# One linear-attention and MLP kernel on one core: reciprocals by a head-major round trip through DRAM, five more tile transposes by DMA, one load for the keys' weight, and a new order of the work

## The chip, the core and the metric

The kernel runs on one core of one Trainium2 chip. The metric is device time in microseconds for one execution; the kernel before took 170.77 us, the median of 3 runs (170.71 to 170.78). The core has five engines with queues of their own: TensorE (PE in the profile, with its weight loads as PEld), VectorE (DVE), ScalarE (ACT), GpSimd (POOL) and SyncE (SP). An engine takes its instructions strictly in the order of the program and waits on semaphores; SP issues all DMAs of this kernel.

## The reference

A block of linear attention with 32 heads of width 16, and behind it a two-layer MLP, both with a layernorm in front and a residual. The sequence has 2048 rows of 512 columns, the MLP is 1792 wide, all data are bfloat16.

```python
def _A_ref(x, wqkv, wo):
    q, k, v = qkv[0], qkv[1], qkv[2]
    phi = lambda t: jnp.where(t > 0, t + 1, jnp.exp(t)) + 1e-6
    pq, pk = phi(q), phi(k)
    kv = jnp.einsum("bhsd,bhse->bhde", pk, v)
    z = jnp.einsum("bhsd->bhd", pk)
    num = jnp.einsum("bhqd,bhde->bhqe", pq, kv)
    den = jnp.einsum("bhqd,bhd->bhq", pq, z)[..., None] + 1e-6
    o = num / den
    return o.transpose(...).reshape(B, S, D) @ wo
...
h = x + _A_ref(_layernorm(x, axis=-1), A_wqkv, A_wo)
h2 = h + _B_ref(_layernorm(h, axis=-1), B_w1, B_w2)    # _B_ref: relu(x @ w1) @ w2
```

## The kernel before

The rows are cut into 16 tiles of 128 (`t`) and 4 blocks of 512 (`c`, four tiles each). Nothing is scheduled by a planner while it builds: the string `ORDER` (lines 18 to 55) lists all steps, a loop at its end (L523) calls `op_<name>` with the numbers behind the name, and each engine runs its part in that order. So `K.4.0` is `op_K(4, 0)`: tile 4, PSUM bank 0. The eight PSUM banks are one tile, `bk`, and the last number of most PE steps names the bank.

The steps, in the order in which they mostly come:

- `lx` loads tiles of x, `lk`, `lq`, `lv`, `lo`, `l1`, `l2` load the weights (L212, L215). `lk.0.2` and `lk.2.2` are the two halves, 256 KB each, of the keys' weight. `warm` (L226) runs PE on zeros.
- Layernorm 1: `S`, `A` (statistics and mean, L229, L230), `R` (1/sqrt by Ln and Exp on ACT), `N` (L243, into `h_nat`).
- A tile must be transposed before it can be multiplied by a weight. It is done either by `T` on PE (four passes against the identity, L262) with a copy out of PSUM by `E` (ACT) or `V` (DVE), or by `X`, a transpose by DMA issued from SP (L283). Before, tiles 0 to 5 go over PE, tiles 6 to 15 by DMA, into `lnT`, one tensor for each block.
- `K` (L291): the keys of a tile, four passes of 512 columns. `F` (exp, L309), `U` (relu, L312), `M` (L316), `D` (L319) make phi of them. `G` (L343) gathers LN(x)^T times phi(k) in four banks over all 16 tiles.
- z, the sum of phi(k) over all rows: `za` (L351) adds tiles 2 to 13 two by two on DVE; `z` (L366) adds the rest on PE, six parts (two for the sum, tiles 0, 1, 14, 15) for each of four blocks of columns, so 24 passes of one column.
- `Q` (L299), `qF`, `qU`, `qM`, `qD`: phi(q), transposed. `kv`, `kx`, `m` make the product of the masked kv and `wo` (L388, L396, L400), so that attention's output is phi(q), scaled by the reciprocals, times `m_sb`.
- The reciprocals, by block: `d4` (L414) makes the denominators, four passes that share the array; row `32 j + h` holds head h (of 8) of column block j. `dl4`, `dx4` (L420, L425) take exp(-ln). Each must then stand on 16 rows, those of its head. For block 0 that is done on PE: `rp` (L430) multiplies by the matrix `erep`, one pass for each of four banks, and `rm` (L436) multiplies out of PSUM. For blocks 1 to 3 it goes through DRAM: `wb` (L442) writes 128 rows of 512 to `scr`, and eight loads `rb` (L445), one for each h, read 4 rows 16 times over into 16 rows of `rr`; then `dm` (L452) multiplies. `rr` exists once, so a block's loads wait until the block before has been multiplied.
- `h` (L461, four passes), `hD` (L467, the residual); layernorm 2 with `s`, `a`, `r`, and `n` (L250), which only subtracts the mean, since 1/sqrt is multiplied in at the end. The transposes of `hn` are again by PE (`t`, L262, with copies `v`) or by DMA (`x`, L284): before, tiles 1, 2, 3 by PE and the others by DMA.
- `p` (L476; `ph`, L485, is half a block) multiplies by w1, `pA` (ACT, L491) and `pD` (DVE, L496) apply relu, `f` (L505) multiplies by w2, `fo` (L513) adds the residual and `fd` (L520) stores.

A DMA waits on SP, so whatever stands behind it in `ORDER` and is issued by SP waits too. DMAs use eight semaphores in turn, and one also waits for that eight DMAs ahead.

Of the kernel before, what the change touches and what calls it, by code (L numbers as in the profile page):

```python
# [15 lines left out]


ORDER = """
table const masks warm.70.7.64 warm.3.7 lx.1.1 S.1 lx.0.1 S.0 lx.3.1 lx.2.1 lx.4.2 A.1 S.3 A.0 R.1.1 R.0.1 S.2
A.3 N.1 A.2 N.0.0.2 N.0.2.2 S.5 R.2.2 T.0.0.0.2 T.0.3.2.2 T.1.1 warm.1.7 E.0.2.2 E.0.0.2 lk.0.2 lk.2.2 N.3  # L20
T.3.3 A.5 S.4 N.2 A.4 lx.6.2 K.0.0 T.2.2 E.1 K.1.1 R.4.2 V.3 F.0.1 U.0.1 F.1.1 U.1.1 V.2 K.2.2 N.4 T.4.0 F.2.1
E.4 M.0.1 N.5 lx.8.4 D.0.1 S.6 S.7 M.1.1 A.6 A.7 D.1.1 S.8 R.6.2 G.0 T.5.1 K.3.3 K.4.0 E.5 G.1 K.5.1 U.2.1
F.3.1 U.3.1 N.7 S.9 A.8 N.6 M.2.1 A.9 M.3.1 D.2.1 R.8.2 lx.12.4 X.7 X.6 F.4.2 U.4.2 G.2 D.3.1 N.8 S.13 N.9
A.13 M.4.2 S.12 D.4.2 A.12 R.12.2 G.3 K.7.3 K.6.2 X.8 X.9 lq.0.2 F.6.2 U.6.2 G.4 K.8.0 S.11 S.10 A.10 N.13
A.11 M.6.2 N.12 K.9.1 R.10.2 U.8.2 F.8.2 D.6.2 X.13 X.12 S.15 N.10 A.15 S.14 A.14 N.11 M.8.2 D.8.2 R.14.2 N.15
N.14 za.4 X.10 X.11 lq.2.2 X.15 X.14 lv.0.2 l1.2.2 lv.2.2 l2.7.7 lo.0.2 lo.2.2 l1.0.2 G.5 G.6 G.7 K.13.1
K.12.0 G.8 K.10.2 K.11.3 F.12.2 U.12.2 F.10.2 U.10.2 Q.0.0.0 Q.0.1.1 G.9 qU.0.0.2 M.12.2 za.6 M.10.2 D.12.2
D.10.2 za.8 za.10 K.14.2 K.15.3 G.10 G.11 G.12 G.13 F.14.2 U.14.2 qF.0.0.2 Q.0.2.0 M.14.2 za.12 D.14.2 G.14 zf
G.15 zhi zlo qM.0.0.2 qD.0.0.2 z.2.2 z.0.2 z.1.2 Q.0.3.1 z.3.2 zc gA.0.2 Q.1.1.3 Q.1.0.2 gD.2.2 qF.0.2.2
qU.0.2.2 qF.1.0.2 qU.1.0.2 kv.2.4 kv.1.4 kv.3.4 kv.0.4 qM.0.2.2 zh qD.0.2.2 qM.1.0.2 kx qD.1.0.2 Q.1.3.1  # L30
Q.1.2.0 qF.1.2.2 m.2.6 m.3.7 d4.0.3 m.0.4 m.1.5 mD.2.2 mD.0.2 Q.2.0.2 dl4.0 dx4.0 qU.1.2.2 Q.2.1.3 rp.0.3.7
rp.0.0.4 rp.0.1.5 rp.0.2.6 Q.2.2.0 Q.2.3.1 qM.1.2.2 rm.0.0.2 rm.0.2.2 h.0.4 qD.1.2.2 hD.0 h.1.5 h.3.7 qU.2.0.2
qU.2.2.2 qF.2.0.2 qF.2.2.2 d4.1.4 h.2.6 dl4.1 dx4.1 Q.3.2.0 Q.3.3.1 s.0 hD.1 a.0 hD.3 s.1 n.0 a.1 hD.2 n.1 s.3
s.2 a.3 qU.3.2.2 qF.3.2.2 x.0 wb.1 rb.1.2 rb.1.4 rb.1.6 rb.1.0 rb.1.7 rb.1.5 rb.1.3 rb.1.1 l2.0.7 a.2 n.3
Q.3.1.3 t.1.5 Q.3.0.2 n.2 v.1 t.3.7 t.2.6 v.3 v.2 ph.0.3.1.0 ph.0.2.0.0 ph.0.3.1.1 ph.0.2.0.1 qF.3.0.2
qU.3.0.2 pA.0.2.2 ph.0.0.2.1 ph.0.0.2.0 ph.0.1.3.1 ph.0.1.3.0 p.0.6.0 p.0.7.1 pD.0.6.2 dm.1.0.2 dm.1.2.2
qM.2.2.2 qM.2.0.2 pA.0.0.2 p.0.5.3 p.0.4.2 p.0.11.1 p.0.10.0 h.6.6 qM.3.0.2 pA.0.4.2 hD.6 h.4.4 h.5.5 p.0.9.3
h.7.7 p.0.8.2 pA.0.8.2 f.2.6.0.7 qD.3.0.2 qD.2.2.2 hD.5 qM.3.2.2 hD.4 s.6 qD.2.0.2 qD.3.2.2 a.6 n.6 hD.7 s.5
s.4 a.4 s.7 a.5 n.4 a.7 p.0.13.3 p.0.12.2 r.0.4 pD.0.12.2 pA.0.10.2 d4.2.0.2 dl4.3 dx4.3 f.0.4.0.7 dl4.2 dx4.2
f.1.5.0.7 n.5 n.7 f.3.7.0.7 f.0.4.7.7 f.2.6.7.7 f.1.5.7.7 x.4 x.7 wb.2 x.5 x.6 p.1.1.1 p.1.0.0 rb.2.0 rb.2.4  # L40
rb.2.6 rb.2.1 wb.3 rb.2.5 fo.0 rb.2.7 rb.2.2 rb.2.3 p.1.2.2 p.1.3.3 pD.1.0.2 p.1.5.1 p.1.4.0 pA.1.4.2 r.4.4
pD.1.2.2 fo.2 dm.2.2.2 dm.2.0.2 f.3.7.7.7 p.1.8.0 p.1.6.2 h.10.6 hD.10 fo.1 fd.1 fo.3 rb.3.6 rb.3.2 rb.3.7
p.1.7.3 h.8.4 pA.1.6.2 p.1.9.1 h.11.7 hD.8 f.4.4.0.7 p.1.10.2 hD.11 s.10 s.11 a.11 n.11 pA.1.8.2 p.1.13.1
h.9.5 hD.9 s.9 a.9 f.7.7.0.7 p.1.11.3 a.10 s.8 rb.3.3 rb.3.0 rb.3.4 rb.3.1 rb.3.5 p.1.12.0 pA.1.10.2 pA.1.12.2
f.5.5.0.7 f.7.7.7.7 n.10 n.9 a.8 r.8.4 x.9 fd.2 dm.3.2.2 dm.3.0.2 n.8 fd.3 fd.0 fo.7 x.8 x.10 x.11 f.6.6.0.7
f.5.5.7.7 h.15.7 fo.5 f.6.6.7.7 p.2.0.0 h.13.5 p.2.1.1 f.4.4.7.7 p.2.2.2 fo.6 pA.2.0.2 p.2.4.0 h.14.6 p.2.3.3
pA.2.2.2 hD.15 hD.13 s.15 fo.4 p.2.5.1 h.12.4 p.2.7.3 pA.2.4.2 p.2.6.2 hD.14 s.13 p.2.8.0 p.2.9.1 hD.12 s.14
a.15 a.13 s.12 a.14 a.12 pD.2.6.2 r.12.4 n.15 pA.2.8.2 n.14 n.13 n.12 x.13 fd.7 fd.6 x.15 fd.5 x.14 x.12
f.11.7.0.7 f.10.6.0.7 f.9.5.0.7 p.2.12.0 p.2.11.3 p.2.10.2 p.2.13.1 pD.2.10.2 pA.2.12.2 f.8.4.0.7 f.9.5.7.7
p.3.0.0 p.3.1.1 f.10.6.7.7 pA.3.0.2 p.3.3.3 p.3.5.1 p.3.4.0 p.3.2.2 pA.3.4.2 f.8.4.7.7 p.3.9.1 pD.3.2.2  # L50
p.3.6.2 p.3.8.0 f.11.7.7.7 p.3.7.3 fo.11 pA.3.8.2 fo.9 fd.4 fo.10 fo.8 p.3.12.0 p.3.13.1 pD.3.12.2 fd.10 fd.9
pA.3.6.2 f.13.5.0.7 p.3.11.3 p.3.10.2 pD.3.10.2 f.12.4.0.7 f.15.7.0.14.0.2 f.12.4.7.7 fd.8 fd.11 f.14.6.0.7
f.13.5.7.7 fo.15.0.2 fo.12 fo.13 fd.12 fd.13 fd.15.0.2 f.14.6.7.7 fo.14 fd.14 f.15.5.0.14.3.1 fo.15.3.1
fd.15.3.1 f.15.4.0.14.2.1 fo.15.2.1 fd.15.2.1
"""


# [1 line left out]
def kernel(  # L59
# [10 lines left out]
    nc = tc.nc  # L70
# [55 lines left out]
    h_nat = big.tile([P, NT, D], BF16, name="h_nat")  # L126
# [16 lines left out]
    mv2 = big.tile([P, NT, nc.vector.BN_AGGR_DIM], F32, name="mv2")  # L143
    rstd2 = big.tile([P, NT], F32, name="rstd2")
    eb = big.tile([P, NE, 2, CW], BF16, name="eb")
    rb = big.tile([P, NE, 2, CW], BF16, name="rb")
    ld = big.tile([P, NCH, CW], F32, name="ld")
    rd = big.tile([P, NCH, CW], BF16, name="rd")
    rr = big.tile([P, KD, CW], BF16, name="rr")
    scr = [dram.tile([KD, Q4, 1, CW], BF16, name=f"scr{c}") for c in range(NCH)]  # L150
    pqs = big.tile([P, NQ, CW], BF16, name="pqs")
    hn = big.tile([P, NQ, D], BF16, name="hn")
    o_t = gT
# [87 lines left out]
    def op_N(t, k=0, n=KD):  # L241
# [106 lines left out]
    def op_za(t):  # L350
# [10 lines left out]

    def op_z(jb, b):
        at_bank["z"] = b
        parts = [zhl[:, i, :] for i in range(2)] + [pk(t)[:, 0, :] for t in range(NT) if not 2 <= t < ZT + 2]
        for i, part in enumerate(parts):
            nc.tensor.matmul(  # L366
                bk[:, b, jb : jb + 1], lhsT=part[:, jb * P : (jb + 1) * P], rhs=ones[:],
                start=(i == 0), stop=(i == len(parts) - 1),
            )
# [131 lines left out]
    def op_f(t, b, f0, n, k=0, w=KD):
# [54 lines left out]
```

## Time and profile before

| | us |
|---|---|
| time, median of 3 runs | 170.77 |
| span of the profiled execution | 169.2 |
| PE busy | 163.5 |
| DVE busy | 101.0 |
| ACT busy | 65.4 |
| load of `wk_sb`, second half, landed | 8.54 |
| first pass of `h.0` starts | 50.16 |
| last DMA landed | 168.40 |

The profile is of one execution; its span is 1.57 us shorter than the median time of the runs, which also holds what lies ahead of the first and behind the last instruction. A group of instructions is shown by line, engine and operation, with its busy time, its count, the mean time of one, and what it waited for. A chain of waits is followed back from the last instruction and then printed in order of time. All times inside the span count from its start.

### The profile page before, as it was taken

The page shows a single profiled execution, that of the slowest core. Times are in us where ns is not written, and L with a number is a line of the kernel's source. Part 1 is how long each engine was busy: PE and PEld are TensorE (multiplying, and loading weights), DVE is VectorE, ACT ScalarE, POOL GpSimd, SP SyncE. Part 2 cuts the span into 40 slices and gives each one's busy share as a digit, 9 for nine tenths or more (in the row PEclk, how much of TensorE's full clock was granted, in tenths as well). Part 3 has the DMA queues.
Part 4 walks back from the last instruction along what each step waited for, and adds up shares of the span by engine and source line. Part 5 has one row for each costly group of instructions (what it writes and reads, how often), then busy time and mean ns, then how long its engine had stood idle before and what let it go on. Part 6 is the DMA issues. An engine that isn't in the chain of part 4 may idle for free.

```text
span 169.2 us, 2376 instructions
## 1 busy us (share of the span) xinstructions
PE 163.5 (97%) x906; PEld 79.9 (47%) x922; DVE 101.0 (60%) x208; ACT 65.4 (39%) x96; POOL 4.7 (3%) x21
## 2 busy tenths in 40 slices
PE   7799999999999999999999999999999999999993
PEld 7454444445534674434444444444444444444643
DVE  3989997896899908895127567326481200255323
ACT  3689766656878672055003222302232112140000
POOL 7300000000000000000000000000000000000000
PEclk9999999999999999999999999999999999999999
DMA  5952656896000246002440031530005500004003
GB/s 135 279 210 50 111 119 153 281 364 259 1 2 4 62 133 208 0 4 59 104 147 2 18 94 48 155 62 0 0 0 97 124 31 0 0 0 127 1 31 93
DMA packets 23163, 15.10 MB, mean 89 GB/s; under 512 B 13808, under 2 KB 22128, under 8 KB 23152
## 3 DMA queue, kind: packets, MB, share of 16 engines
q1 hardware_dynamic: 23152, 14.95, 31.3%
q8 instruction: 7, 0.11, 0.3%
q14 instruction: 4, 0.03, 0.1%
HBM read 9.44 MB, written 2.49 MB: 70 GB/s over the span
## 4 chain that ended last, share of the span: by engine, by line
PE 91%; DMA 3%; SPq 1%; issue 1%; DVE 1%
PE bk L505 29%; PE bk L476 26%; PE bk L343 8%; PE bk L461 8%; PE bk L291 8%; PE bk L299 7%; DMA wk_sb<-in_A_wqkv_dram 3%; PE bk L485 2%; SPq L212 1%; PE bk L262 1%; DVE pqs L436 1%; PE bk L414 1%; PE bk L400 1%; PE bk L388 1%; PE bk L366 0%
## 5 line engine op out<-in xcount | busy, mean ns | idle before, releaser
L505 PE MATMUL bk<-w_sb,at 128*128 128x512 bf16 (+2 forms) x248 | 50.7, 355 | 0.2
L476 PE MATMUL bk<-lnT,w_sb 128*128 128x512 bf16 x203 | 47.9, 379 | 0.2
L491 ACT ACTIVATE at<-bk 128x1024 bf16<-128x1024 f32 x19 | 19.2, 1023 | 64.7 <-PE bk L476 57.4
L505 PEld LDWEIGHTS <-at 128*128 128x128 bf16 x252 | 23.5, 98 | 25.3 <-issue 0.4
L476 PEld LDWEIGHTS <-w_sb 128*128 128x128 bf16 x208 | 20.4, 98 | 24.3
L496 DVE TENSOR_SCALAR at<-bk 128x1024 bf16<-128x1024 f32 x9 | 11.0, 1219 | 26.7 <-PE bk L476 26.7
L513 DVE SCALAR_TENSOR_TENSOR gT<-bk,rstd,h_nat 128x512 bf16<-128x512 f32 (+2 forms) x18 | 12.1, 689 | 21.6 <-PE bk L505 19.2
L309 ACT ACTIVATE eb<-bk 128x1024 bf16<-128x1024 f32 (+1 forms) x18 | 16.6, 928 | 5.8 <-PE bk L291 4.3
L312 ACT ACTIVATE rb<-bk 128x1024 bf16<-128x1024 f32 (+1 forms) x18 | 16.4, 925 | 2.8 <-PE bk L299 2.4
L467 DVE TENSOR_TENSOR h_nat<-bk,x_nat 128x512 bf16<-128x512 f32 x16 | 10.9, 684 | 9.6 <-PE bk L461 9.5
L461 PE MATMUL bk<-m_sb,pqs 128*128 128x512 bf16 x63 | 15.9, 379 | 0.3 <-DVE pqs L436 0.2
L291 PE MATMUL bk<-wk_sb,lnT 128*128 128x512 bf16 x62 | 15.3, 379 | 0.2 <-DMA wk_sb<-in_A_wqkv_dram 0.2
L299 PE MATMUL bk<-lnT,wq_sb 128*128 128x512 bf16 x62 | 15.2, 379 | 0.1
L343 PE MATMUL bk<-at,h_nat 128*128 128x512 bf16 x55 | 13.2, 379 | 0.1
L229 DVE BATCH_NORM_STATS2 st<-x_nat 128x6 f32<-128x512 bf16 x16 | 10.6, 677 | 1.8 <-DMA x_nat<-in_A_x_dram 1.8
L231 DVE BATCH_NORM_STATS2 st<-h_nat 128x6 f32<-128x512 bf16 x16 | 10.6, 680 | 0.1
L461 PEld LDWEIGHTS <-pqs 128*128 128x128 bf16 x64 | 6.1, 98 | 8.0 <-DVE pqs L436 0.7
L343 PEld LDWEIGHTS <-h_nat 128*128 128x128 bf16 x64 | 6.2, 98 | 7.3
L291 PEld LDWEIGHTS <-lnT 128*128 128x128 bf16 x64 | 6.1, 98 | 7.4 <-issue 0.5
L299 PEld LDWEIGHTS <-wq_sb 128*128 128x128 bf16 x64 | 5.9, 98 | 6.6 <-issue 0.2
L316 DVE TENSOR_SCALAR eb<-eb 128x1024 bf16<-128x1024 bf16 (+1 forms) x18 | 6.8, 386 | 2.1 <-ACT eb L309 2.1
L235 ACT ACTIVATE rstd<-mv,eps 128x2 f32<-128x2 f32 (+2 forms) x13 | 3.8, 295 | 7.0 <-DVE mv L230 4.7
(67 smaller groups left out, 99.6 us busy)
## 6 DMA issues: line engine op xcount, KB each, us to landing
w_sb<-in_B_w_dram SPq DMA_DIRECT2D x4, 896.0 KB, 6.9
out_dram<-gT SPq DMA_DIRECT2D x15, 128.0 KB, 1.9
rr<-scr SPq DMA_DIRECT2D x24, 64.0 KB, 2.7
x_nat<-in_A_x_dram SPq DMA_DIRECT2D x2, 512.0 KB, 6.4
x_nat<-in_A_x_dram SPq DMA_DIRECT2D x4, 128.0 KB, 2.2
x_nat<-in_A_x_dram SPq DMA_DIRECT2D x2, 256.0 KB, 4.5
wk_sb<-in_A_wqkv_dram SPq DMA_DIRECT2D x2, 256.0 KB, 4.5
wq_sb<-in_A_wqkv_dram SPq DMA_DIRECT2D x2, 256.0 KB, 2.9
```

The source lines that it names most:

```text
L291: nc.tensor.matmul(bk[:, b, :], lhsT=lnT[c][:, kd, j * P : (j + 1) * P], rhs=wk_sb[:, kd, :], start=(kd == 0), stop=(kd == KD - 1),)
L299: nc.tensor.matmul(bk[:, b, :], lhsT=wq_sb[:, kd, j * P : (j + 1) * P], rhs=lnT[c][:, kd, :], start=(kd == 0), stop=(kd == KD - 1),)
L309: nc.scalar.activation(out=buf(eb, kind, i, n), in_=bank(at_bank[kind, i], n), func=ACT.Exp)
L312: nc.scalar.activation(out=buf(rb, kind, i, n), in_=bank(at_bank[kind, i], n), func=ACT.Relu)
L343: nc.tensor.matmul(bk[:, KD + kd, :], lhsT=ln_nat[:, t, kd * P : (kd + 1) * P], rhs=pk(t)[:, 0, :], start=(t == 0), stop=(t == NT - 1),)
L461: nc.tensor.matmul(bk[:, b, :], lhsT=pqs[:, (c * KD + jb) % NQ, j * P : (j + 1) * P], rhs=m_sb[:, jb, :], start=(jb == 0), stop=(jb == KD ...
L467: nc.vector.tensor_tensor(out=h_nat[:, t : t + n, :], in0=bank(at_bank["h", t], n), in1=x_nat[:, t : t + n, :], op=ALU.add,)
L476: nc.tensor.matmul(bk[:, b, :], lhsT=w1_sb[:, kd, f * P : (f + 1) * P], rhs=lnT[c][:, kd, :], start=(kd == 0), stop=(kd == KD - 1),)
L491: nc.scalar.activation(out=acts[c % 2][:, f : f + n, :], in_=bank(at_bank["p", c, f], n), func=ACT.Relu)
L496: nc.vector.tensor_scalar(out=acts[c % 2][:, f : f + n, :], in0=bank(at_bank["p", c, f], n), scalar1=0.0, scalar2=None, op0=ALU.max,)
L505: nc.tensor.matmul(bk[:, b, 0 : w * P], lhsT=acts[c % 2][:, f, j * P : (j + 1) * P], rhs=w2_sb[:, f, k * P : (k + w) * P], start=(f == 0), ...
L513: nc.vector.scalar_tensor_tensor(out=o_t[:, t % NO, cols], in0=bk[:, at_bank["f", t, k], 0 : w * P], scalar=rstd2[:, t : t + 1], in1=h_nat ...
```

## The change

- Reciprocals: block 0 also goes through DRAM (`wb.0`, `rb.0`, `dm.0` for `rp` and `rm`). `scr` becomes head-major, `[32, 4, 512]`: `wb` writes row `32 j + h` to place `(h, j)`, as 4 x 32 x 512, and one `rb` for a block reads 8 heads, each 4 x 512 in one run of 4 KB, 16 times over into all 128 rows of `rr` (512 KB).
- Transposes: LN1 tiles 4 and 5 by DMA (`X`), so 12 tiles; LN2 tiles 0, 1, 2 of the first block by DMA (`x`), only tile 3 on PE.
- `lk.0.4`: the keys' weight in one load of 512 KB; `lq.0.4`: the queries' too, and ahead of x tiles 8 to 15.
- z: `za.2.1` also takes tiles 0 and 1, so `z` has four parts and 16 passes.
- `n` now makes mean minus h instead of h minus mean, and `pA`, `pD` multiply by -1 ahead of relu. `op_nA` does the same on ACT and is not in the order.
- The order is new from end to end; `h` and LN2 of all tiles come earlier against `p` and `f`, `rb` of block 2 stands ahead of the transposes of block 1, and the last tiles end in another order.

PE issues 892 passes instead of 922; SP issues 71 DMAs instead of 88, 20 of them less for `rb`.

```diff
-table const masks warm.70.7.64 warm.3.7 lx.1.1 S.1 lx.0.1 S.0 lx.3.1 lx.2.1 lx.4.2 A.1 S.3 A.0 R.1.1 R.0.1 S.2
+table const masks warm.70.7.64 warm.2.7 lx.2.1 S.2 lx.0.1 S.0 lx.1.1 A.2 lx.3.1 S.1 lx.4.2 R.2.1 lk.0.4 A.0 S.3
...
+G.10 zhi qU.1.0.2 qF.1.0.2 G.13 G.8 G.11 G.12 zlo z.3.2 z.1.2 z.0.2 z.2.2 qM.1.0.2 zc G.9 zh d4.0.1 G.15 G.14
+qD.1.0.2 dl4.0 Q.1.2.2 dx4.0 wb.0 Q.1.3.3 gA.0.2 gD.2.2 kv.0.1 kv.1.1 qF.1.2.2 kv.2.1 kv.3.1 kx qM.1.2.2 Q.2.3.5
+qU.1.2.2 Q.2.0.0 rb.0.0.8 l2.0.7 qD.1.2.2 m.0.6 m.1.7 m.3.3 m.2.2 d4.1.4 mA.0.2 Q.2.1.1 mA.2.2 dm.0.0.2 dm.0.2.2
+h.0.7 hD.0 s.0 dl4.1 qF.2.0.2 dx4.1 a.0 h.1.2 hD.1 n.0 Q.2.2.4 qU.2.0.2 qU.2.2.2 wb.1 l1.2.2 qF.2.2.2 h.2.3 s.1
...
+qM.2.2.2 qM.3.2.2 qD.2.0.2 ph.0.3.1.1 ph.0.2.0.1 ph.0.1.3.1 qD.2.2.2 qD.3.2.2 pD.0.2.2 p.0.7.5 d4.2.6.2 rb.1.0.8
+ph.0.0.2.1 dl4.2 p.0.6.4 dm.1.2.2 dm.1.0.2 p.0.4.0 h.6.1 pD.0.6.2 pD.0.0.2 hD.6 h.7.6 h.4.5 hD.7 s.6 h.5.4 s.7
+p.0.5.1 dl4.3 hD.5 a.7 a.6 s.5 p.0.12.6 dx4.2 wb.2 rb.2.0.8 n.6 a.5 hD.4 p.0.9.3 n.7 x.6 s.4 n.5 a.4 p.0.10.4
+p.0.8.2 dx4.3 pA.0.4.2 dm.2.2.2 dm.2.0.2 n.4 pD.0.8.2 p.0.11.5 pD.0.10.2 f.3.0.0.7 h.8.1 hD.8 x.7 x.5 p.0.13.7
+pD.0.12.2 wb.3 x.4 h.11.2 s.8 r.4.4 h.9.3 rb.3.0.8 l2.7.7 hD.11 h.10.1 a.8 hD.9 p.1.11.6 p.1.10.5 hD.10 dm.3.2.2
+dm.3.0.2 s.9 s.10 s.11 p.1.1.4 p.1.0.3 a.9 a.10 pA.1.10.2 a.11 h.12.6 n.8 hD.12 n.9 pA.1.0.2 s.12 p.1.7.5
...
-    scr = [dram.tile([KD, Q4, 1, CW], BF16, name=f"scr{c}") for c in range(NCH)]
+    scr = [dram.tile([Q4, KD, CW], BF16, name=f"scr{c}") for c in range(NCH)]
...
-            out=hn[:, t % NQ, :], in0=h_nat[:, t, :], scalar1=mv2[:, t, 0:1], scalar2=None,
-            op0=ALU.subtract,
+            out=hn[:, t % NQ, :], in0=h_nat[:, t, :], scalar1=-1.0, scalar2=mv2[:, t, 0:1],
+            op0=ALU.mult, op1=ALU.add,
...
-    def op_za(t):
-        nc.vector.tensor_tensor(out=zacc[:], in0=pk(2, 2) if t == 4 else zacc[:], in1=pk(t, 2), op=ALU.add)
+    def op_za(t, first):
+        prev = pk(t - 2, 2) if first else zacc[:]
+        nc.vector.tensor_tensor(out=zacc[:], in0=prev, in1=pk(t, 2), op=ALU.add)
+        summed.update(range(t - 2 if first else t, t + 2))
...
     def op_wb(c):
-        nc.sync.dma_start(out=scr[c].rearrange("j h o n -> (j h) (o n)"), in_=rd[:, c, :])
+        nc.sync.dma_start(out=scr[c].rearrange("h j n -> j h n"), in_=rd[:, c, :])
...
-    def op_rb(c, h):
+    def op_rb(c, h, n):
         nc.sync.dma_start(
-            out=rr[h * DH : (h + 1) * DH, :, :],
-            in_=scr[c][:, h, :, :].rearrange("j o n -> o j n").broadcast_to([DH, KD, CW]),
+            out=rr[h * DH : (h + n) * DH, :, :],
+            in_=scr[c][h : h + n, :, :].rearrange("h (o j) n -> h o (j n)", o=1).broadcast_to([n, DH, KD * CW]),
         )
...
-            out=acts[c % 2][:, f : f + n, :], in_=bank(at_bank["p", c, f], n), func=ACT.Relu
+            out=acts[c % 2][:, f : f + n, :], in_=bank(at_bank["p", c, f], n), func=ACT.Relu, scale=-1.0
...
-            scalar1=0.0, scalar2=None, op0=ALU.max,
+            scalar1=-1.0, scalar2=0.0, op0=ALU.mult, op1=ALU.max,
```

## The prediction

> **What bounds the kernel.** I read the busy shares, the forty slices, the chain of waits, then the instructions in order of time around 46 to 51 us, and the DMA list.
>
> ```profile
> PE 163.5 (97%) x906; PEld 79.9 (47%) x922; DVE 101.0 (60%) x208; ACT 65.4 (39%) x96; POOL 4.7 (3%) x21
> ...
> PEclk9999999999999999999999999999999999999999
> ...
> PE 91%; DMA 3%; SPq 1%; issue 1%; DVE 1%
> ```
>
> PE is busy throughout at full clock, and the chain runs 91% over it: only fewer PE passes, or fewer gaps between them, shorten the span. The chain's own pieces price a pass.
>
> ```profile
> 46.44 1.73 PE bk L299 x8
> 48.16 0.38 PE bk L430 x4
> 48.55 0.06 DVE pqs L436
> 48.61 1.07 issue
> 49.68 1.23 DVE pqs L436
> 50.90 0.05 issue
> 50.95 2.33 PE bk L461 x10
> ```
>
> Eight 512-column passes take 1.73 us: 0.216 each, 0.863 for a group of four. The DVE pieces look like a 2.4 us wait, but are not: PE ran eight Q passes and two passes of `h.0` beside them, as the timeline shows:
>
> ```profile
> 48.43 1.90 PE L299 MATMUL bk<-lnT,wq_sb 128*128 128x512 bf16 x7
> 50.16 0.59 PE L461 MATMUL bk<-m_sb,pqs 128*128 128x512 bf16 x2
> 50.95 2.33 PE L461 MATMUL bk<-m_sb,pqs 128*128 128x512 bf16 x10 [0.19 <-DVE pqs L436]
> ```
>
> The second pass starts at 50.38, so PE was free at 50.59 and stood 0.36 us. Start to start, I find only two other real waits after 8 us: 0.34 for `wk_sb` at 8.2 and 0.12 for `lnT` at 20.9. So little idle time is left to win.
>
> **What the change takes from PE.** After the first K group, in order of the program:
> - Tiles 4 and 5 no longer transposed on PE, and tile 2's now before K: 12 transposes, 0.22 per four (chain): 0.67.
> - LN2 tiles 1 and 2 by DMA, eight transposes: 0.45.
> - No `rp`: 0.38, and 0.20 of gaps at its two ends: 0.58.
> - z over 16 one-column passes instead of 24 (18 took 0.43): 0.19.
> - The waits of 0.36 and 0.12 go.
> - Against this, the two K passes that ran on the first half of `wk_sb` at 7.80 now wait for the whole load: -0.43. The second half landed at 8.54 behind the same bytes, so I let the whole land then; 0.4 either way.
>
> Sum: 1.94 us less. DVE loses two 1.22 us multiplications (L436) and gains two of 0.68 (L452); the added `mult` in `n`, `pA`, `pD` keeps shape and source, so their rows (0.34, 1.02, 1.22) stand, and DVE also gains one `za` sum (1.22) and loses the two copies that emptied tiles 1 and 2 (0.42 each); it has idle time in the stages where these lie. SP issues 17 DMAs fewer (71 for 88). The whole load of `wq_sb` (512 KB) now stands ahead of x tiles 8 to 15; two 256 KB pieces took 1.4 and 0.8 there, so these tiles land 2.2 us later, near 12.8 and 14.2; by the rows in front of it on DVE, S.8 is due near 13: nothing, with little to spare.
>
> **What it puts on the path.**
>
> *LN1 by DMA.* K.4 is due after K.0 to K.3 and four Q groups: 8.5 + 8 x 0.863 = 15.4. Four DMA transposes occupy SP for 5.22 us (timeline), 1.3 apart, and land 2.5 after issue; K.7, due 2.6 after K.4, needs the fourth, 6.4 after the first issue. So `X.5` must leave by 11.6. It waits for N.5, in front of which DVE now has S.6 (its tile landed at 9.31, behind the same bytes), A.5, S.7, A.6, M.0 and A.7: 9.35 + 2 x 0.60 + 3 x 0.09 + 0.27 + 0.35 = 11.44. That is 0.1 of spare on an estimate good to some tenths. Bounds 0 and 1.0; I take 0.2, nearer to the sum.
>
> *Reciprocals of block 0 by DMA.* New chain: d4.0 (visible after 0.40), Ln 0.68, Exp 0.63, write `wb.0`, load `rb.0`, a DVE multiplication 0.68, then `h.0`; with 0.03 to 0.04 per handover it is 2.6 + w + l after d4.0 starts. PE has beside it d4.0 0.43, G.15 and G.14 1.73, five Q groups 4.32, kv 0.89, m 0.86, d4.1 0.5: 8.7 us. The room for w + l is thus 6.1; I take 5.9, since the second multiplication, 0.6 behind, is needed 0.43 behind. Queued behind `h.0` on PE is everything else.
>
> *The last block's.* `wb.3` stands on SP behind the transposes x.6, x.7, x.5, and these behind hD, s, a, n. From rb.1's landing: two multiplications 1.32; then DVE's pD x2, hD x3, s x3, a x2, n, 7.24 less 0.084 overlap each: 6.3; three transposes 3.9; w + l; two multiplications 1.36: 12.9 + w + l. PE starts h.6 at 1.36 and has 19 groups of 0.863 and seven passes of f (1.51) up to h.12: 19.27. Room: 6.4. rb.1 itself lands with almost nothing to spare, rb.2 with about 0.8.
>
> *What w and l are.* Rows:
>
> ```profile
> out_dram<-gT SPq DMA_DIRECT2D x15, 128.0 KB, 1.9
> rr<-scr SPq DMA_DIRECT2D x24, 64.0 KB, 2.7
> ...
> wq_sb<-in_A_wqkv_dram SPq DMA_DIRECT2D x2, 256.0 KB, 2.9
> ...
> scr<-rd SPq DMA_DIRECT2D x3, 128.0 KB, 1.9
> ...
> out_dram<-gT SPq DMA_DIRECT2D x1, 64.0 KB, 1.7
> out_dram<-gT SPq DMA_DIRECT2D x2, 32.0 KB, 1.5
> ```
>
> If the new transfers are spread like these, w = 1.9, and l for 512 KB lies between 2.9 (256 KB) and the first 896 KB weight load, 4.72 from issue to landing: 2.94 + 0.4 x 1.78 = 3.65. Then w + l = 5.55 and neither room is overrun. Lower bound: a 64 KB load, 1.9 + 2.7 = 4.6. Upper bound: the eight loads of block 1 carry the same 512 KB and took 6.1 from the first issue (58.47) to the last landing (64.61): 8.0.
>
> But the shapes are new. Every copy of the kernel before begins on both sides with a dimension of 128 or 16; `wb` now writes 4 x 32 x 512 and `rb` reads 8 heads x 16 copies x 2048. The stores above grow 0.4 us for 96 KB, 240 GB/s, where one engine carries
>
> ```profile
> 34.50:38.50 4.00, 3.95 (x19) 1.77 (x19) 3.93 (x7) 1.68 (x2) 0.00 (x0) 1.00 1.10 364
> ```
>
> 364 / 16 = 22.8 GB/s when all are busy (last column GB/s, before it the DMA share). So transfers with 128 rows in front are spread wide. If a copy is divided along its first dimension only, `wb` gets 4 engines with 32 KB each (1.44 us, against 0.36) and `rb` 8 with 64 KB (2.88, against 1.44): w = 2.98, l = 5.09, together 8.07, next to the upper bound. I take this: it is the division by rows that all earlier shapes fit, and the write and the load both lead with a small dimension.
>
> The Trainium skill (DMA: Bandwidth & Descriptors, "Why a DMA increments its semaphore by 16 and not by 1") says that the number of engines is the largest up to 16 that divides the slowest dimension of both sides. By it, the write takes 4 engines and the load 8, as in the case just priced. No transfer of before has a front dimension that 16 does not divide, so its trace cannot show it; the time by the rule is that of the forecast, and by even spreading that of the first rival.
>
> Waits by 8.07: at h.0 8.07 - 5.9 = 2.2; at h.12 8.07 - 6.4 = 1.7.
>
> **Sum** against the profiled execution (span 169.2; the median of the runs, 170.77, holds 1.6 us around it that I leave alone): -1.94 + 0.2 + 2.2 + 1.7 = +2.1. Span 171.3, time **172.9 us**.
>
> **Rivals.**
> 1. *Spread over all 16 engines (ends on the other side).* w + l = 5.55 fits both rooms. What is late next: x.0 and x.1 stand in the queues behind the 896 KB load l1.2 (4.72 alone), and the first `ph` passes, which PE reaches about 0.5 earlier than they land, wait. -1.94 + 0.2 + 0.5 = -1.2: 169.5. For it: nothing in the trace shows a narrow transfer. Against it: the shapes. It decides at w + l of 7.0: there the waits of 1.1 and 0.6 take the whole gain.
> 2. *Only one of the two is narrow.* Write alone: 6.63, waits 0.7 and 0.2, -0.8, 169.9. Load alone: 6.99, waits 1.1 and 0.6, 0.0, 170.8.
> 3. *The early stage is late as well.* N.5 a further 1 us behind, then K.4 to K.7 wait as much: forecast +0.8, 173.7. For it: DVE stands at 9 tenths from slice 3 on. Against it: K.0 to Q.0.2 give DVE 6.9 us before the first tile is due.
>
> **Chances.** Forecast 0.63, with early lateness (rival 3) 0.09, rival 1 0.18, rival 2 0.10. Likeliest one's own range: w + l from 7.3 to 9.0 gives waits of 2.3 to 5.7, so +0.6 to +4.0: 171.4 to 174.8. The whole range goes down to rival 1: 169.3 to 174.8. About 0.2% (0.34 us) is what a measurement of this kernel can tell from no change. Faster by more: rival 1 but its edge and the half of rival 2 with a narrow write, 0.22; within: the other half and that edge, 0.06; slower: the forecast and rival 3, 0.72.
>
> **What would show it.** Right: the landing of `scr<-rd` near 3.0 us and of `rr<-scr` near 5.1; PE idle before `h.0` of about 2 us put down to DVE `pqs` of the multiplication by `rr`, and again before h.12; only four PE transposes after the first K, and no passes over `erep`. Wrong: landings of 1.9 and 3.6, and no PE gap over 0.5 us from 9 us on; then rival 1 holds. If the landings are short and the time still grows, the gap is in the K and Q groups between 12 and 30 us.

## The result, and the profile after

The changed kernel takes 186.69 us (median of 4 runs, 185.02 to 187.21) against 170.78 for the kernel before on the same chip: 9% slower, a ratio of 1.091 [1.0863, 1.0957]. The forecast was 172.9. The profiled execution took 186.86 us, with a span of 185.1, 15.9 longer than the span of before. (It transposes 27 tiles by DMA where the kernel before transposes 23: four more, not the five of the title.)

The page after, the same three lines that carried the page before (busy time, granted clock in forty slices, shares of the chain that ended last):

```profile
PE 166.6 (90%) x876; PEld 79.2 (43%) x892; DVE 101.5 (55%) x207; ACT 63.0 (34%) x96; POOL 4.7 (3%) x21
...
PEclk9999999999988999999975999999999999999999
...
PE 46%; DMA 7%; DVE 1%; issue 0%; SPq 0%
```

PE has fewer passes and is yet 3.1 us longer busy, at 90% of its span instead of 97%. The clock row, flat before, has two dents, from slices 12 and 21 on. The chain names DMA second, though it reaches back only to 81.83 us; its pieces around the second dent say which transfers (start, us, what):

```profile
83.15 3.33 DMA scr<-rd
86.48 0.02 issue
86.50 8.21 DMA rr<-scr
94.71 0.02 issue
94.73 1.30 DVE pqs L456 x2
96.04 0.05 issue
96.08 1.89 PE bk L465 x4
```

The write takes 3.33 us, the load 8.21, both multiplications wait behind it, and then four passes of `h.12`, which took 0.86 before, take 1.89. The list of waits (engine, line, waited for: us, times, longest) has the same pair:

```profile
DVE pqs L456 <- DMA rr<-scr: 14.4, 4, 6.5
...
PE bk L465 <- DVE pqs L456: 11.0, 3, 5.3
```

From the landings and the PE starts in the trace (start to start, less the pass), the PE waits of after are: 5.45 us before `h.0` (48.65 to 54.32), 5.18 before `h.12` (90.69 to 96.08), 1.45 at the half-block passes, 1.02 in the K groups (0.62 at K.4, 0.19 at K.6, 0.21 at K.10), 0.90 before `h.6`. The clock costs more behind the two long ones. The windows around the first show it (window, us, PE busy, weight loads, DVE, ACT, POOL, then granted clock, DMA share and GB/s), and two more those around the second:

```profile
50.53:53.94 3.41, 0.00 (x0) 0.00 (x0) 0.37 (x1) 1.67 (x3) 0.00 (x0) 1.00 1.07 197
53.94:57.35 3.41, 3.03 (x8) 1.05 (x9) 1.93 (x4) 0.00 (x0) 0.00 (x0) 0.50 0.82 311
57.35:60.76 3.41, 3.41 (x17) 1.54 (x16) 3.34 (x9) 1.94 (x2) 0.00 (x0) 1.00 0.29 80
...
91.49:94.90 3.41, 0.00 (x0) 0.00 (x0) 0.17 (x1) 0.64 (x1) 0.00 (x0) 1.00 1.01 178
94.90:101.72 6.82, 5.41 (x13) 2.01 (x15) 5.68 (x16) 0.80 (x3) 0.00 (x0) 0.50 0.11 38
```

A stretch of 3.41 us without one pass, then 3.41 us at half clock with 8 passes where 17 follow in the next. The second wait is followed by 6.83 us at half clock (94.90 to 101.72). Half of what PE was busy there is lost: (57.35 - 54.32) / 2 + (101.72 - 96.08) / 2 = 4.3 us.

The sum closes within 0.5: -1.94 (the passes taken away, as forecast) + 1.02 + 5.45 + 1.45 + 0.90 + 5.18 + 4.3 = +16.4, measured +15.9.

### The profile page after: what moved, and what is told of

It is laid out like the page before. It is cut to its first block, busy times and chain, and to the rows that moved or that the text cites. A ratio compares the mean times of both kernels' runs of the same rounds, so it can differ in the third digit from the quotient of the medians.

```text
span 185.1 us, 2310 instructions
## 1 busy us (share of the span) xinstructions
PE 166.6 (90%) x876; PEld 79.2 (43%) x892; DVE 101.5 (55%) x207; ACT 63.0 (34%) x96; POOL 4.7 (3%) x21
## 4 chain that ended last, share of the span: by engine, by line
PE 46%; DMA 7%; DVE 1%; issue 0%; SPq 0%
PE bk L509 25%; PE bk L480 18%; DMA rr<-scr 4%; PE bk L465 3%; DMA scr<-rd 2%; DVE pqs L456 1%; DVE gT L517 1%; DMA lnT<-hn 0%; DVE hn L248 0%; SPq L287 0%; SPq L446 0%
## 5 line engine op out<-in xcount | busy, mean ns | idle before, releaser
L509 PE MATMUL bk<-w_sb,at 128*128 128x512 bf16 (+2 forms) x245 | 50.0, 355 | 0.4
L480 PE MATMUL bk<-lnT,w_sb 128*128 128x512 bf16 x205 | 48.7, 388 | 0.3 <-issue 0.2
L495 ACT ACTIVATE at<-bk 128x1024 bf16<-128x1024 f32 x15 | 15.3, 1023 | 52.9 <-PE bk L480 27.7
L465 PE MATMUL bk<-m_sb,pqs 128*128 128x512 bf16 x64 | 17.8, 428 | 11.0 <-DVE pqs L456 11.0
L500 DVE TENSOR_SCALAR at<-bk 128x1024 bf16<-128x1024 f32 x13 | 15.7, 1222 | 8.6 <-PE bk L480 8.3
L465 PEld LDWEIGHTS <-pqs 128*128 128x128 bf16 x64 | 6.6, 107 | 21.2 <-DVE pqs L456 13.0
L294 PE MATMUL bk<-wk_sb,lnT 128*128 128x512 bf16 x63 | 14.8, 380 | 0.7 <-DMA lnT<-h_nat 0.5
L456 DVE TENSOR_TENSOR pqs<-pqT,rr 128x1024 bf16<-128x1024 bf16 x8 | 5.2, 689 | 14.4 <-DMA rr<-scr 14.4
```

Of the source, the lines that this page charges most:

```text
L294: nc.tensor.matmul(bk[:, b, :], lhsT=lnT[c][:, kd, j * P : (j + 1) * P], rhs=wk_sb[:, kd, :], start=(kd == 0), stop=(kd == KD - 1),)
L465: nc.tensor.matmul(bk[:, b, :], lhsT=pqs[:, (c * KD + jb) % NQ, j * P : (j + 1) * P], rhs=m_sb[:, jb, :], start=(jb == 0), stop=(jb == KD ...
L480: nc.tensor.matmul(bk[:, b, :], lhsT=w1_sb[:, kd, f * P : (f + 1) * P], rhs=lnT[c][:, kd, :], start=(kd == 0), stop=(kd == KD - 1),)
L495: nc.scalar.activation(out=acts[c % 2][:, f : f + n, :], in_=bank(at_bank["p", c, f], n), func=ACT.Relu, scale=-1.0)
L500: nc.vector.tensor_scalar(out=acts[c % 2][:, f : f + n, :], in0=bank(at_bank["p", c, f], n), scalar1=-1.0, scalar2=0.0, op0=ALU.mult, op1= ...
L509: nc.tensor.matmul(bk[:, b, 0 : w * P], lhsT=acts[c % 2][:, f, j * P : (j + 1) * P], rhs=w2_sb[:, f, k * P : (k + w) * P], start=(f == 0), ...
```

## The experiments

**Theory A**: the new write and load are divided along their small first dimension, 4 and 8, over as few engines, and the round trip no longer fits the room in front of `h.0` and `h.12`. Rivals: **B**, the 896 KB weight load issued right behind `rb.0` and `rb.3` takes their bandwidth; **C**, reading a row 16 times is slow by itself; **D**, the new order is slow by itself. All kernels are edits of the changed one.

### lone: the transfers by themselves

Behind the last store, each transfer waits for the one before, but for the second changed write, which left 0.7 us behind the second load without repeats; the computation stays.

```diff
+y.0 y.1 y.2 y.3 y.4 y.5 y.0 y.6 y.4 y.1 y.2 y.5 y.6 y.0 l2.0.7
# y.0 rb as changed | y.1 512 KB, 128 rows in front | y.2 512 KB, 8 in front, no row twice
# y.3 one head, 64 KB | y.4 32 rows x 4 copies | y.5 wb as changed | y.6 128 rows written
```

> The changed kernel, with transfers added behind its last store, each waiting for the one before: the load as changed (8 heads x 16 copies x 2048), a load of the same 512 KB with 128 rows in front, a load with 8 in front that repeats no row, the load of one head (64 KB), a load of 32 rows x 4 copies, the write as changed (4 x 32 x 512), a write of 128 rows. Its time says nothing. Theory A (a copy is divided only by the first dimension of both its sides, so the changed load runs on 8 DMA engines and the write on 4): lone, both loads with 8 in front take 5.0 to 6.3 us from issue to landing, those with 128 or 32 in front 3.3 to 3.9, the write with 4 in front 3.3, that with 128 rows 1.9. Rival C (reading a row many times over is what is slow): the two loads that repeat rows take 5 or more, the two that do not 3.3 to 3.9. Rival B (the load of 896 KB issued right behind is what made it 8.2): all loads of 512 KB take 3.3 to 3.9 here, except the last one of the changed form, which has such a load behind it.

From issue to the last landing: the load as changed 6.37 and 6.88 us; the same bytes with 128 rows in front 3.09 and 3.19; 8 in front without repeats 6.23 and 6.53; 32 rows by 4 copies 4.05 and 3.93; one head 2.69; the write as changed 3.29 (7.02 for the second, beside that load), with 128 rows 1.70. Since each of the first ones waits for the one before, SyncE's row shows it as the distance of the starts: 6.44 for the changed load, 3.10 for the wide one, 6.25 for the one without repeats.

```profile
182.01 0.64 SPq L450 DMA_DIRECT2D rr<-scr  x1
188.45 0.34 SPq L533 DMA_DIRECT2D rr<-in_B_w_dram  x1
191.55 0.65 SPq L536 DMA_DIRECT2D rr<-in_B_w_dram  x1
197.80 0.59 SPq L450 DMA_DIRECT2D rr<-scr  x1
```

The order is the one that A expects, with figures up to 0.6 us off its ranges. C falls as the main cause: the load without repeats takes nearly as long. A smaller cost of repeating is not excluded, since 32 rows by 4 copies take 0.7 to 1.0 longer than 128 rows without; but these two also read different tensors. The last load, with 896 KB issued behind it, took 7.80, about 1.2 more than without: B has a share. The trace also shows the division: a wide transfer leaves 16 semaphore events near its end, the changed load 8 and a single one about 1 us after issue, the changed write 4 and one. And it shows where the estimate of the load went wrong. Each of the 8 engines moves 16 packets of 4 KB at a mean of 249 ns, 16.4 GB/s, where the wide load's take 170 and the forecast went by 22.8 GB/s (180); that is 4.0 us instead of 2.9. The first packet starts 1.4 after issue and the last landing is 0.9 behind the last packet, 2.3 together, near the 2.2 that the forecast's sum leaves for it. In the profile after, beside the 896 KB load, the packets took 328 and 322 ns: 5.2 us.

### warm_waits: PE kept busy in the two waits

```diff
-h.0.7 hD.0
+warm.22.7 h.0.7 hD.0
-a.11 h.12.6
+a.11 warm.20.6 h.12.6
```

> The changed kernel with 22 passes of 512 columns into an unused bank ahead of h.0 and 20 ahead of h.12, so that PE works in the two waits instead of standing. If PE's idle time of over 5 us is what halved the granted clock for 3.4 and 6.8 us behind the waits: clock 1.00 to the end, the waits as long as before (h.0 and h.12 start within 0.5 us of the changed kernel's, relative to what precedes them), time down by 3.5 to 4.5, to 182.2 to 183.2 us. If the lower clock has another cause, or costs nothing because other engines set the pace there: 186.7 us within 0.5.

182.13 us, 1.0667 [1.0639, 1.0695], clock 1.00 to the end. With passes on zeros in them the two waits last as long as before (5.7 and 5.1 us), and the kernel is 4.6 us shorter, against 4.3 for the half clock from the windows. The two figures agree in part by luck, since other waits moved too: x.2 is no longer late, so the 1.45 us at the half-block passes are gone, and the wait before `h.6` grew from 0.90 to 1.85. The cleaner reading is behind `h.12`, where nothing else waits: from its first pass to the end it is 86.3 us instead of 89.0, so 2.7, against 2.8 from the windows.

### no_behind: the weight loads taken from behind the round trips

```diff
-rb.0.0.8 l2.0.7
+rb.0.0.8
-rb.3.0.8 l2.7.7
+rb.3.0.8
-lv.0.2
+lv.0.2 l2.0.7 l2.7.7
```

> The changed kernel with both halves of w2 loaded before the first reciprocal is written, so that no load of 896 KB stands behind rb.0 and rb.3. Theory A: these two land in 6.3 us, as rb.2 did with transposes alone behind it, instead of 8.1 and 8.2, the waits before h.0 and h.12 shorten from 5.4 and 5.2 to about 3.6 and 3.3, and the clock is lowered for less time: 178.5 to 182.5 us. Rival B: they land in 3.9 or less, both waits stay under 1 us, about 172 us. Rival D (the new order, not the transfers, costs the time): 186.7 within 1 us.

182.34 us, 1.0661 [1.0614, 1.0707]. The loads take 6.66 to 6.74 us, all four alike, instead of 6.3 to 8.2, and the waits fall to 4.10 and 3.62. So B is worth 1.4 to 1.6 us at each of the two places, and the larger part of the waits stays without it, as A expects. (The profiled run was the longest of this kernel, 185.27; its clock stood at half for 6.83 us behind each wait.)

### wide_load: the load leads with 32 rows

The mask that makes the denominators repeats each head four times, so `rd` holds 32 rows for each column block, and the load needs 4 copies instead of 16. The write stays 4 x 32 x 512.

```diff
-        keep(mask_h[:], mask_h[:], [[0, KD], [-DH, Q4]], 0, 1)
-        keep(mask_h[:], mask_h[:], [[0, KD], [DH, Q4]], DH - 1, -1)
+        for q in range(KD):
+            cols = mask_h[:, q, :].rearrange("p (h r) -> p h r", r=KD)
+            keep(cols, cols, [[-DH, Q4 // KD], [0, KD]], 0, 1)
+            keep(cols, cols, [[DH, Q4 // KD], [0, KD]], DH - 1, -1)
...
-            out=rr[h * DH : (h + n) * DH, :, :],
-            in_=scr[c][h : h + n, :, :].rearrange("h (o j) n -> h o (j n)", o=1).broadcast_to([n, DH, KD * CW]),
+            out=rr[:],
+            in_=scr[c].rearrange("h (o j) n -> h o (j n)", o=1).broadcast_to([Q4, KD, KD * CW]),
```

> The changed kernel with mask_h changed so that d4 makes each head's denominator four times (32 columns = 8 heads x 4 copies, where 24 were zero); the load then reads 32 rows x 4 copies x 2048 and leads with 32. The write still leads with 4. Theory A: l falls to 3.6 to 4.6 us (the higher figure where the 896 KB load runs beside it), w stays 3.3; w + l of 6.9 to 7.9 gives waits of 1.0 to 2.0 and 0.5 to 1.5, too short to lower the clock: 173 to 176 us. Rival C: l stays at 6 to 8 us and the time at 186.7 within 1.5 us.

172.42 us, 1.0099 [1.008, 1.0118]. The list of DMA issues has the load (KB each, median us to landing):

```profile
rr<-scr SPq DMA_DIRECT2D x4, 512.0 KB, 3.6
```

The waits are 1.13 before `h.0` and 0.56 before `h.12`, the clock stays at 1.0, and the time is below the 173 to 176 expected. The shape of one load makes 14.3 of the 15.9 us between the two kernels; A holds. To D, the order by itself, are left at most the 1.9 us that this kernel is still above the one before.

### wide_both and eight_loads: both wide, and the transfers of before

`wide_both` writes a plain 128 x 512 into a `scr` with the column block in front, and loads it as four pieces that each lead with 32 rows. `eight_loads` has the old write and the old eight loads in the new order.

```diff
# wide_both
-        nc.sync.dma_start(out=scr[c].rearrange("h j n -> j h n"), in_=rd[:, c, :])
+        nc.sync.dma_start(out=scr[c].rearrange("j h n -> (j h) n"), in_=rd[:, c, :])
...
+        for j in range(KD):
+            nc.sync.dma_start(
+                out=rr[:, j, :],
+                in_=scr[c][j].rearrange("h (o n) -> h o n", o=1).broadcast_to([Q4, KD, CW]),
+            )
```

> The order of the changed kernel, with the reciprocals' rows made four times over by a wider mask, so that the write is a plain 128 x 512 and the load four pieces that each lead with 32 rows. Theory A (narrow division costs the time): the write takes 1.7 to 1.9 us, the four pieces about 3.9 from the first issue to the last landing, together 5.6 to 5.8, which fits the rooms of 5.9 and 6.4; the waits before h.0 and h.12 are 0.3 at most. The waits at K.4 (0.9) and at the first half-block passes (1.25) stay. Time 1.5 us under the 172.42 of the kernel with only the load widened: 170.9 to 171.2. Theory D (the new order itself is slow): the gaps close but as much opens elsewhere, 172 or more.

> The new order with the transfers of the kernel before: a write of 128 rows, then eight loads of 64 KB, one for each head, leading with 16 rows. Theory A: write 1.7 to 1.9, eight loads 6.1 from first issue to last landing, together 8.0; waits 2.1 before h.0 and 1.6 before h.12, too short for the clock to fall; with the waits at K.4 (0.9) and the half-block passes (1.25) and 1.94 less work this is +3.9: 174.5, 174.0 to 175.5. If not the narrowness but the round trip in this order costs the time (D), the waits are near 5 and the clock falls: 185 to 187.

`wide_both`: 172.9 us, 1.0114 [1.007, 1.0158], no faster than with the narrow write, so the expectation missed. The write fell to 1.7 to 2.4 us; the four pieces took 4.3 to 5.5 instead of 3.9. The wait before `h.0` is 0.37, but the one before `h.12` is 1.24: two pieces of `rb.3` land 3.6 and 3.9 after issue, the two ahead of them 2.4 and 2.9. Half-block passes still wait 1.24. What makes single transfers late became the next question.

`eight_loads`: 178.34 us, 1.0388 [1.0315, 1.0462]. Write and loads take 42.62 to 50.72, 8.1 us, which is the 8.07 of the forecast. The waits are 2.5 and 2.0, near the 2.2 and 1.7 that it derived. Yet the time is 5.4 above the forecast, and the expectation missed as well. The span's sum: -1.94 + 1.20 (K.4 and later K) + 2.53 (h.0) + 1.08 (half-block passes) + 0.75 (h.6) + 2.02 (h.12) + 1.8 (half clock) = +7.4, as measured (176.6 - 169.2). The half clock came after a wait of only 2.4 us (2.53 with a second short one behind it):

```profile
48.73:52.14 3.41, 1.20 (x6) 0.31 (x4) 1.15 (x2) 3.41 (x6) 0.00 (x0) 1.00 0.69 206
52.14:55.56 3.42, 3.42 (x9) 1.20 (x9) 2.08 (x5) 0.56 (x1) 0.00 (x0) 0.50 0.98 318
```

PE was busy 1.20 of the 3.41 us ahead of it, about a third. The wait of 2.0 before `h.12`, which the 3.41 us grid cuts in two, brought no half clock. Nor does each execution pay: of the four, the mean clock was 0.99 in two, 0.98 in the longest (179.49) and 1.00 in the shortest (176.52). The windows stand elsewhere in each execution (an edge at 52.14 here, at 53.94 in the profile after), so a wait of this length may fall into one window or be split over two.

### weights_early and x12_behind: taking bytes away in front of the transposes

On `wide_both`. The first moves the three 896 KB loads to the stretch around 30 us where the queues stand idle; the second also puts the load of x tiles 12 to 15 behind X.5 and X.4.

```diff
# weights_early
-wb.1 l1.2.2
+wb.1
...
-lv.0.2
+lv.0.2 l1.2.2 l2.0.7 l2.7.7
# x12_behind, on top
-lx.12.4 X.5 qF.0.0.2 Q.0.3.1 X.4 A.8
+X.5 qF.0.0.2 Q.0.3.1 X.4 lx.12.4 A.8
```

> The kernel with both transfers wide, and the three 896 KB loads of the MLP's weights issued behind the last load of wv, in the stretch where the DMA queues stand idle. If the transposes x.0 to x.2 were late because l1.2.2 was in front of them in the queues: they land 2.5 after issue, the wait of 1.25 us at the first half-block passes falls to 0.3 or less, and the time is about 1 us under the kernel with both transfers wide: 169.8 to 170.2, under the kernel before. If something else holds them (n.1, n.2 late on DVE): the wait stays and the time with it.

> As the one before, and the 512 KB load of x tiles 12 to 15 issued behind the transposes X.5 and X.4 instead of ahead of them, with the statistics of these tiles later on DVE. If X.5 landed 4.0 us after its issue because of the bytes ahead of it in the queues: it lands about 2.5 after, K.4's wait of 0.8 to 0.9 us falls to 0.2 or less, and the time is 0.5 to 0.8 us under the kernel with the weights early, 169.0 to 169.6. If tiles 12 to 15 then come too late for K.12 (at 27 us) or the statistics block DVE, a new gap between 16 and 30 us takes it back.

`weights_early`: 172.66 us, 1.0105 [1.0077, 1.0132]. x.0 and x.1 now land 2.45 and 2.41 after issue (4.66 and 3.57 in `wide_both`), as expected, but x.2 lands 4.11 after its own, and the half-block passes wait 1.63: no gain, and the expected 169.8 to 170.2 was missed.

`x12_behind`: 175.19 us, 1.0254 [1.0205, 1.0303]. X.5 lands 2.50 after issue, as expected. But X.6 and X.7, issued behind the 512 KB, land at 18.79 and 19.27, K.6 waits 2.27 us, and the clock stands at half from 19.25 to 22.66. The bytes were moved from in front of two transposes to in front of the next two, and the expected 169.0 to 169.6 was missed.

### code_later20 and code_later10: moving the fetches of PE's code

The queue part of the page has seven packets of 16 KB of kind "instruction". In each trace so far a transfer was late where one of them was under way. In the profile after it is x.2. The DMA answer over the window from its issue to its landing, 63.1 to 67.1 (kind, packets, MB, share; then the issues):

```profile
q8 instruction: 1, 0.02, 2.1%
...
lnT<-hn SPq DMA_TRANSPOSE x1, 3.9
```

**Theory E**: PE's own code comes over the same DMA engines, one block every 256 instructions, and what is in flight then lands late. Fewer warm-up passes ahead of everything, with the same number of columns, move the fetches against the work. On `weights_early`:

```diff
-warm.70.7.64
+warm.50.7.90      # code_later20
+warm.60.7.75      # code_later10
```

> The kernel with the weights early, with 50 warm-up passes of 90 columns in place of 70 of 64 (the same 4500 columns, so the same time), hence 40 instructions fewer on PE ahead of everything. Theory E: the transfers that are late now (x.2, landing 4.1 us after issue against 2.4 for its neighbours; the last two pieces of rb.3, 3.6 and 3.3 against 2.4) were in flight while a 16 KB block of PE's instructions was fetched over the same DMA engines, as the packets of the instruction queue show at 11.6, 58.4 and 80.0 us; a block is fetched every 256 instructions, so 40 instructions fewer move the fetches 20 passes later, to about 16, 61 and 83. Then x.2 lands 2.45 after issue and the wait of 1.6 us at the half-block passes goes to 0.2 or less, and the wait of 0.6 before h.12 goes; other transfers are hit in their place (X.7 or X.9 near 16, the last pieces of rb.1 near 61), which cost up to 1.0. Time 1.2 to 2.2 us under the 172.66 of the kernel with the weights early: 170.4 to 171.5. If x.2 was late for another reason (its place in the queue, n.2), its landing stays at 4 after issue and the time at 172.4 to 172.9.

> As the one before with 60 warm-up passes of 75 columns: 20 instructions fewer on PE, fetches 10 passes later: about 13.7, 59.5 and 81. Theory E: x.2 lands just ahead of the fetch, 2.45 after issue, and the wait at the half-block passes goes; the first fetch falls on X.4 or X.6 and may cost 0.5 to 1.0 at K.4 to K.6; the fetch at 81 may still catch the last piece of rb.3. Time 170.6 to 171.9. Otherwise 172.4 to 172.9.

`code_later20`: 171.51 us, 1.0051 [1.0036, 1.0066]. The fetches at 37.0, 58.4 and 80.0 moved to 41.5, 60.7 and 85.6; x.2 lands 2.38 after issue and the wait is gone. In its place three pieces of `rb.1` are in flight at 60.7 and land 3.6 to 4.2 after issue instead of 2.3 to 2.5, and `h.6` waits 0.67. The first fetch did not move (11.4), against the expectation.

`code_later10`: 170.97 us, 1.0019 [1.0003, 1.0035], some 0.2% above the kernel before, barely clear of no difference. In `weights_early` the weight loads of the half-block passes wait for x.2 (first line, from its list of waits); here 20 such passes run without a break (from the timeline), since x.2 lands 2.39 after issue, 0.15 ahead of the fetch at 58.8:

```profile
PEld L492 <- DMA lnT<-hn: 1.7, 1, 1.7
```

```profile
57.89 2.35 PE L492 MATMUL bk<-lnT,w_sb 128*128 128x256 bf16 x20
```

E holds: nothing was changed but the number and the width of the warm-up passes, and the delay went to other transfers (here three pieces of `rb.1`, 3.2 to 3.6). The places of the fetches bear it out: in all eight kernels with 892 weight loads the last three come at weight load 589, 716 and 840, within one, some 125 passes and as many loads apart; with 20 fewer ahead they come later in time and at nearly the same loads (599, 721, 842).

### g_first and g0_first: work in front of K.4

What is left in `code_later10` is 0.55 at K.4, 0.19 at K.6, 0.20 at K.10, 0.22 before `h.0`, 0.49 before `h.6`, 0.24 before `h.12`. (The expectation below also counts 0.23 at K.5, which is a pass whose record is missing.) Two tries at the first:

```diff
# g_first, on code_later10 (G.0 G.1 and qF.0.2.2 qU.0.2.2 leave their later places)
-N.8 S.15 K.4.6 A.14
+N.8 S.15 qF.0.2.2 qU.0.2.2 G.0 G.1 K.4.2 A.14
# g0_first
-warm.70.7.64 warm.2.7
+warm.58.7.78 warm.4.7
...
+N.8 D.3.1 S.15 qF.0.2.2 qU.0.2.2 G.0 K.4.2 A.14
```

> The kernel with both transfers wide, the weights early and the fetches 10 passes later, and with the eight passes of G.0 and G.1 put ahead of K.4 (K.4 to K.7 then use banks 2, 3, 0, 1, and exp and relu of the third and fourth Q group come before those of K.4). The waits of 0.55, 0.23 and 0.19 at K.4 to K.6 are there because X.5 lands at 14.3, with the first fetch at 11.5 and the x tiles' 512 KB ahead of it in the queues; with 1.73 us of passes in front that wait for nothing, they go: about 0.9 us less, 169.9 to 170.3, under the kernel before. If K.4's later start makes exp, relu and the additions behind it the bound, a gap opens between 19 and 30 us and takes some of it back: 170.5 to 171.

> As the one before, but only G.0 (four passes, 0.86 us) ahead of K.4, so that exp and relu behind K.4 start no later than they did with the wait; the addition D.3 ahead of the third Q group's exp, whose buffer it reads; and four wide warm-up passes in place of two with 58 of 78 columns ahead of them, so that PE stands less between 4.8 and 6.2 us and the clock does not fall at 8.6 as it did there (3.4 us at half, some 1.7 us lost). The waits at K.4 to K.6 (0.97 together) go but for 0.1 to 0.3, nothing opens between 19 and 32 us: 169.9 to 170.4, ratio 0.996 to 0.999. If the additions of the early tiles on DVE are the bound, the three waits of 0.42 near 30 us stay: 170.8 or more.

`g_first`: 171.73 us, 1.0036 [1.0013, 1.0059]. In it the addition of phi(k) of tile 3 reads a buffer that the third Q group's exp and relu have already filled, so this tile's phi is another's; all instructions are there. The waits at K.4 and K.6 are gone, but three of 0.42 to 0.45 opened near 30 us, for later transposes by DMA: what DVE normalises for them stands behind its work on the later exp of K.4. In the profiled run the clock was also at half from 8.61 to 12.02, behind a window in the warm-up in which PE stood for some 40%.

`g0_first`: 172.27 us, 1.0067 [1.0041, 1.0094]. K.4 no longer waits for its tile, but K.4 and K.6 now wait for their banks, 0.43 and 1.63, which ACT has to empty of the Q groups (engine, line, waited for: us, times, longest):

```profile
PE bk L296 <- ACT rb L317: 1.7, 2, 1.5
```

The expectation missed: this stage is bound by ACT and DVE as well, and passes put ahead only move the wait. No version beat the kernel before.

## Why the prediction was wrong, point by point

- **PE work taken away, -1.94**: right as a sum, to about 0.5. With this number the sums of waits and clock close within 0.5 us in each trace worked through: `wide_load` +2.1 against +1.9 measured, `wide_both` +1.8 and +1.8, `eight_loads` +7.4 and +7.4, `weights_early` +1.5 and +1.4, `code_later10` 0.0 and -0.3. One of its terms has the wrong sign: the whole `wk_sb` landed at 7.62, not 8.54, and the four passes of K.0 ended at 8.52, 0.5 ahead of before (9.01) instead of 0.4 behind. As the sum closes all the same, something of like size is missing elsewhere in it; where was not found.
- **The division, 4 and 8 engines**: right, by the 4 + 1 and 8 + 1 semaphore events. The Trainium skill (DMA: Bandwidth & Descriptors, "Why a DMA increments its semaphore by 16 and not by 1") says that the issuing engine writes the counts of the unused engines at once; the single event about 1 us after issue agrees, ahead of the first landing.
- **The rooms, 5.9 and 6.4**: right. With the measured w + l of 11.43 and 11.56, 11.43 - 5.9 = 5.5 and 11.56 - 6.4 = 5.2, measured 5.45 and 5.18.
- **The term l, 5.09: the step that failed first.** It was 8.10 and 8.21 at the two places, 6.7 without a load behind it, 6.4 to 6.9 alone. The price used a rate from a stretch with all 16 engines busy and spread it to 8, and did not count the 896 KB that the new order issues right behind; the first is worth about 1.6 (6.7 against 5.09), the second 1.4 to 1.6. w = 2.98 was near (3.31 and 3.33). So each wait was 3.3 to 3.5 us longer than forecast, +6.7 together.
- **The clock, at nothing: the second failure.** At 5 us a wait also costs what follows it: 4.3 us by the windows, of which `warm_waits` confirms the second part directly (2.7 for 2.8). A forecast wait of 2.2 seemed no matter for the clock; `eight_loads` shows that one of 2.4 can be enough. The Trainium skill (TensorE: Matmul & The Clock Gate, "What's actually happening") has free-running windows of 3413 ns; the stretches of 3.41 and 6.83 us agree. The same page of the Trainium skill ("HAM oscillation — how this bites in real kernels") asks for no idle gaps above about 3.4 us. The runs show less to be enough: in `eight_loads` a gap of 2.4 us, in a window that was two thirds idle.
- **K.4, taken at 0.2 with bounds 0 to 1.0**: 0.62 at K.4 and 0.19 at K.6, inside the bounds. PE was there at 14.57, not 15.4, since K.0 had begun early. X.5 left at 10.35, earlier than the 11.44 worked out, but held SyncE for 2.2 us instead of 1.3 and landed 4.07 behind issue instead of 2.5; X.4, for which K.4 waits, so left only at 12.65 and landed at 15.15. In front of X.5 were the x tiles' bytes, with a code fetch at 11.1 beside it. `x12_behind` took the bytes away (X.5 landed in 2.50), but its fetch came at 9.9, so the shares of the two are not separated. Rival 3 expected such a wait, but from a late N.5.
- **The half-block passes**: the forecast had nothing there, rival 1 had 0.5 behind `l1.2`. After: 1.45, from x.2 and a code fetch. Where the round trip is short, `l1.2` costs 1.25, as rival 1 said, at more than twice its size.
- **rb.1 with almost nothing to spare**: it took 7.22 us, with x.2 and a code fetch (64.1) beside its start, and `h.6` waited 0.90.

Even with w + l as forecast the time was 178.3 (176.5 to 179.5), not 172.9: `eight_loads` is that case. So of the 13.8 us between forecast and result some 8 come with the longer load and its clock, and some 5 were missing whatever its size: 1.8 of clock behind a wait of the right length, and waits in places that the forecast held at next to nothing.

What is open: why a narrow transfer's packets are slower on each engine (249 ns against 170, and 230 for the narrow one that repeats no row) than those of a wide one; it was not tried apart. Why the first code fetch did not move is not known either.

## What to carry to other kernels

Look at the first dimension of both sides of a transfer before its bytes: 512 KB took 3.1 us with 128 rows in front and 6.2 with 8, and a mask that makes the rows four times over gave it back. Price a wait on PE with the clock behind it: half of the next 3.4 or 6.8 us, once about two thirds of a 3.4 us window are idle. And where a transfer must land on time, leave it 1 to 2 us for a code fetch; where in the order that fetch falls depends on the number of PE instructions ahead of it.

## What the runs showed of the hardware beyond that

- The clock can be read window by window, on the 3.41 us grid that its changes give. In the traces whose grid is known, each of the eight windows at full clock in which PE was busy at most 38% was followed by one at half clock; of those with 50% or more none was, but for one in the warm-up of `g_first` (60%, narrow passes). A window at half clock with PE busy 44 to 72% was followed by a second, one with 89% or more by full clock.
- Seven code fetches of 16 KB fall into every execution. Where x.2 or pieces of `rb` were in flight beside one, they landed 1.2 to 1.9 us late (2.4 to 4.1 for x.2, 2.4 to 3.6 up to 4.2 for pieces of `rb`). Not every fetch costs: in the profile after `rb.3` took 8.21 with one under way and `rb.0` 8.10 without, and a store beside the last fetch landed in the usual 1.9. The Trainium skill (Runtime: NRT & Kernel Launch, "Instruction fetch mechanics") gives blocks of 16 KiB, 256 instructions, fetched over a DMA queue, and calls their cost mostly hidden. The count agrees: 1784 passes and weight loads in 7 blocks. For PE no wait on a fetch shows in these traces; for a transfer with no slack the fetch is not hidden.
- A load issued behind another slowed the one ahead, 6.7 to 8.1 us, and its packets from 254 to 258 ns in `no_behind` to 322 to 328 in the profile after. The two seem to share few engines meanwhile: of the 16 landing events of the 896 KB load behind `rb.0`, eight come 7.7 to 8.1 us after issue, as `rb.0` ends, and eight at 9.4 to 9.7. That fits eight engines free for it from the start and eight that turn to it after `rb.0`. What the slower packets wait for is not shown.
